# Splitting the loads of x into two 48-row parts and reordering the transform's exchanges, in a fused Fourier, gated and expert-routed kernel

## Chip, cores and metric

One core of a Trainium2 chip runs the kernel. The metric is the device time of one launch, in microseconds (us). Three runs of the kernel before give a median of 3674.27 us.

## What is computed

Three layers follow each other on 8 sequences of 3072 positions with 256 channels each. The first is a Fourier transform along the positions, a complex product with two 256 x 256 matrices, a soft threshold, and the inverse transform:

```python
X = np.fft.rfft(x, axis=1)
Yr = Xr @ w_r - Xi @ w_i + b_r
Yi = Xr @ w_i + Xi @ w_r + b_i
Yr = sign(Yr) * maximum(abs(Yr) - 0.01, 0); Yi likewise
y = np.fft.irfft(Yr + 1j * Yi, n=3072, axis=1)
```

The second is a gated layer on all 24576 tokens, `sigmoid(y @ w_gate) * (y @ w_val) @ w_out`, with an inner width of 1536. The third sends each token whose skip score is above zero to one of 8 experts, chosen by the largest of 8 logits, and adds `gate_w * (relu(z @ w1[e]) @ w2[e])` to it; the other tokens pass through.

## The kernel before

Every matmul operand is a pair of 16-bit halves (a high and a low part), so a product takes three matmuls. The scale of each pair is a power of two found from a maximum: `allpow` takes the maximum of each partition on VectorE, spreads it over the partitions with one small matmul on TensorE (L169, tile `pm`), and reduces that on VectorE.

The forward transform of one sequence is done in two stages. In the first stage the 3072 positions are seen as 48 rows (n) by 64 columns; the 64 columns are two halves (h) of 32, taken 4 at a time, which makes 8 chunks. `load` (L485) brings one chunk of x, 384 KB, into a tile of 96 partitions (2 halves x 48 rows) with 1024 numbers each. The source pattern of this one transfer has the half h outermost, then the 48 rows, then 1024 numbers. For each chunk, `bound` takes the maximum, `scale` and `halve` make the 16-bit pair, `cols` runs the first transform matmuls with the constant `c1` (printed as `c`), and the result `ah` goes to the DRAM buffer `asc` (L524). There are three buffers for chunks of x, so the load of chunk c+3 can be issued once chunk c is used up.

The second stage works on one frequency group at a time. `fetch` (L591) reads 128 KB of `asc` into `al`: 4 parts (r), each with 32 positions (j) of 512 numbers. `freq`, `mix` and `inv` transform, mix and transform back, and `store` (L764) writes 128 KB of the same form to `zsc`. Both exchanges have r outermost and j next: partition r x 32 + j of the tile holds part r, position j. The inverse first stage, `y_gen`, loads chunks `zt` of `zsc` (L799, 384 KB, 96 partitions) and makes `yT`, on which the gated layer works (`moe_gen`, L870 and L903).

All of these transfers are issued in program order by one queue, SP's. The only others here are a few constants on ScalarE's queue and the indirect ones on GpSimd's.

The first sequence (b = 0) is transformed alone, before the gated layer can start; this stretch is called the boot here. Beside it the weights of the gated layer are prepared (`setup_moe_gen`: tiles `raw`, `cm`, `cv`, `wf`, `wgv`, `wo`; the loads of `raw` are L324 and L328). At the end of the boot's transform the kernel issues the first three loads of x for sequence 1, then the first `zt` load, then the next `raw`. After the boot the gated layer's matmuls set the pace, and the transforms of sequences 1 to 7, the routing and the preparation of the experts' weights run as steps of generators between them. `step` runs one step: first what the step before left in `k.late` (among others the matmul and the reduction of `allpow`), then the step's own instructions. The program order is fixed when the kernel is built.

Of the kernel before, what the change touches and what calls it, by code (L numbers as in the profile page):

```python
# [17 lines left out]
N1, N2, NK, HN = 48, 64, 24, 32  # L18
# [17 lines left out]
def make_consts():  # L36
    n1, n2, k1, k2 = (np.arange(v, dtype=np.float64) for v in (N1, N2, NK, 64))

    def hl(a):
        a = np.asarray(a, np.float64) * 64.0  # L40
        hi = a.astype(np.float16)
        lo = (a - hi.astype(np.float64)).astype(np.float16)
        return hi, lo

    th = 2 * np.pi * (((64 * n1[:, None, None] + n2[None, :, None]) * k1) % SEQ) / SEQ
    c1 = np.zeros((2, N1, HN, 2, 2, NK))
    c2 = np.zeros((2, 2, NK, HN, 2, N1))
    w = 4.0 / 3.0
    alt = np.stack([n1 * 0 + 1, 1 - 2 * (n1 % 2)])
    for h in range(2):  # L50
        t = th[:, h * HN:(h + 1) * HN]
        c1[h, :, :, 0, h, :] = np.cos(t)
        c1[h, :, :, 1, h, :] = -np.sin(t)
        c2[0, h, :, :, h, :] = (w * np.cos(t)).transpose(2, 1, 0)
        c2[1, h, :, :, h, :] = (-w * np.sin(t)).transpose(2, 1, 0)
        c1[h, :, :, :, h, 0] = alt.T[:, None, :]
        c2[:, h, 0, :, h, :] = w / 2 * alt[:, None, :]
    c1 = np.stack(hl(c1.reshape(96, HN, 96)), 2)
    c2 = np.stack(hl(c2.reshape(96, HN, 96)), 2)
    ph = 2 * np.pi * ((n2[:, None] * k2) % 64) / 64  # L60
    co, si = np.cos(ph), np.sin(ph)
    sg = np.where(k2 < 32, 1.0, -1.0)
    fx = np.zeros((2, 64, 2, 64))
    for r, (re, im) in enumerate(((co, -si), (si, co))):
        fx[r, :, 0] = re
        fx[r, :, 1] = sg * im
    fi = np.zeros((2, 64, 2, 64))
    fi[0, :, 0] = co.T
    fi[0, :, 1] = si.T
    fi[1, :, 0] = -sg[:, None] * si.T  # L70
    fi[1, :, 1] = sg[:, None] * co.T
    su = np.zeros((2, 64, 128))
    sv = np.zeros((2, 64, 128))
    si = np.zeros((128, 2, 64))
    rows = [(0, 0, q) for q in range(33)] + [(1, 0, q) for q in range(32)]
    rows += [(0, 1, q) for q in range(1, 32)] + [(1, 1, q) for q in range(32)]
    for i, (odd, im, q) in enumerate(rows):
        t = 2 * np.pi * (((24 * odd + 48 * q) * n2) % SEQ) / SEQ
        f = 1.0 if odd == 0 and q in (0, 32) else 2.0
        su[odd, :, i] = -np.sin(t) if im else np.cos(t)  # L80
        sv[odd, :, i] = np.cos(t) if im else np.sin(t)
        si[i, odd] = f * (-np.sin(t) if im else np.cos(t))
    f2 = np.stack([np.stack(hl(m.reshape(128, 128)), 1) for m in (fx, su, sv, fi, si)], 1)
    return {
        "c1": np.ascontiguousarray(c1),
        "c2": np.ascontiguousarray(c2),
        "f2": np.ascontiguousarray(f2),
    }
# [13 lines left out]
def shape_consts():  # L102
    c = make_consts()
    q = np.arange(CT)
    cc = np.arange(NC)
    row = 64 * ((q % 192) // 4)[None, :] + HN * (q // 192)[None, :] + NJ * cc[:, None] + (q % 4)[None, :]
    slot = CT * cc[:, None] + q[None, :]
    ids = np.stack([row, slot], -1).reshape(NC * NT3, 128, 2).transpose(1, 0, 2)
    c["ids"] = np.ascontiguousarray(ids.astype(np.float32))
    p = np.arange(128)  # L110
    first = p[:, None] < np.array([65, 64])
    chk = [(p % HN)[:, None] // NJ == cc[None, :], first, ~first]
    c["chk"] = np.concatenate(chk, 1).astype(np.float32)
    m16 = np.zeros((128, 3, 128), np.float16)
    m16[:, 0] = p[:, None] < p[None, :]
    m16[:, 1] = 1.0
    m16[:, 2] = np.eye(128)
    c["m16"] = m16
    c["m32"] = np.eye(128, dtype=np.float32)
    r = np.zeros((128, 2 * NE + 1 + NBLK), np.float32)  # L120
    r[:, :NE] = np.arange(NE, 0, -1)
    r[:, NE:2 * NE] = np.arange(NE) * NTOK
    r[:, 2 * NE] = p
    r[:, 2 * NE + 1:] = np.arange(NBLK)
    c["rc"] = r
    return c
# [34 lines left out]
def allpow(k, out, in_, lo):  # L161

    p = k.pt.tile([128, 1], F32, tag="pp", name="pp", bufs=6)
    pow2(k, p, in_, lo)

    def spread():
        ps = k.pa.tile([128, 512], F32, tag="pa", name="pm")[:, :128]
        w = p.bitcast(BF16)[:, 1:2].broadcast_to([128, 128])
        k.nc.tensor.matmul(ps, w, k.idb, start=True, stop=True)  # L169
        k.V.tensor_reduce(out, ps, axis=AX.X, op=ALU.max)  # L170

    k.late.append(spread)


def absmax(k, out, in_, axis=AX.X):
# [30 lines left out]
    k.G.tensor_tensor(lo, tmp, hi, op=ALU.subtract)  # L206


def step(k, r):

    k.V.sum = k.S.sum = k.T.sum = k.G.sum = 0.0
    todo, k.late = r[1], []
    for f in todo:
        f()
    got = next(r[0], -1)
    r[1] = k.late
    if got == -1 or isinstance(got, str):
        for f in r[1] if got == -1 else ():
            f()
        return got  # L220
    return max(k.V.sum + k.G.sum, k.S.sum)


def run_all(k, gen):
    r = [gen, []]
    while step(k, r) != -1:
        pass

# [226 lines left out]
def attn_gen(k, b):  # L455
# [23 lines left out]
    def load(i):  # L479

        e, c = b + i // NC, i % NC
        if e < NB:
            xv = k.d.x[e].rearrange("(n h j) d -> h n j d", h=2, j=HN)
            x32[e, c] = k.xp.tile([96, NJ, D], F32, tag="x32", name=f"x32_{e}_{c}")
            nc.sync.dma_start(x32[e, c], xv[:, :, c * NJ:(c + 1) * NJ, :])  # L485

    def bound(c, h=None):
        if h is None:
# [98 lines left out]
    def fetch(g):  # L587
        al = als[g] = k.wp.tile([128, 2, 2, D], F16, tag="al", name=f"al_{b}_{g}", bufs=AL)
        for i, k1 in enumerate(groups[g]):
            src = asc.rearrange("(r q) j l e -> q r j (l e)", r=4)[k1]  # L590
            nc.sync.dma_start(al[:, i].rearrange("p l e -> p (l e)"), src)  # L591

    for g in range(AL):
# [155 lines left out]
    def inv(g):  # L749
        W, yh = len(groups[g]), yhs.pop(g)  # L750
        ps = bank()
        for n, (a, w) in enumerate(PROD):
            k.T.matmul(
                ps[:, :W * D].rearrange("p (a e) -> p a e", a=W), k.f2[:, 4 if g == 0 else 3, a, :], yh[:, :W, w, :],
                start=n == 0, stop=n == 2,
            )
        zh = k.wp.tile([128, 2, 2, D], F16, tag="zh", name="zh")
        pv = ps[:, :W * D].rearrange("p (a e) -> p a e", a=W)

        def store():  # L760
            (split_far if b == 0 else split)(k, zh[:, :W, 0, :], zh[:, :W, 1, :], pv, 2.0**-13)
            for i, k1 in enumerate(groups[g]):
                dst = zsc.rearrange("(r q) j l e -> q r j (l e)", r=4)[k1]
                nc.sync.dma_start(dst, zh[:, i].rearrange("p l e -> p (l e)"))  # L764

        if b == 0:
            k.late.insert(0, store)
        else:
            store()
# [74 lines left out]
def y_boot(k):  # L844
    for c in range(2):
        yield from y_gen(k, 0, c, True)
# [410 lines left out]
def build(tc, d, nb=NB, nstat=NSTAT, dbg=None):  # L1257
# [18 lines left out]
    k.tc, k.nc, k.d, k.nstat = tc, nc, d, nstat  # L1276
    k.due, k.folded = None, False
    k.V, k.S, k.T, k.G = (Meter(e, r) for e, r in ((nc.vector, 960.0), (nc.scalar, 1200.0), (nc.tensor, 2400.0), (nc.gpsimd, 960.0)))
    k.yT, k.st, k.zsc, k.R, k.late = {}, {}, {}, {}, []
    k.x32, k.zt = {}, {}  # L1280
    with ExitStack() as top, tc.manual_schedule():

        def P(name, bufs, space=None, ctx=top, side=None):
            kw = {} if space is None else {"space": space}
            if side is not None:
                kw["side"] = side
            if space is not bass.MemoryType.DRAM:
                kw["reuse_waits"] = "tile"
            return ctx.enter_context(tc.tile_pool(name=name, bufs=bufs, **kw))
# [14 lines left out]
        k.xp = P("xp", 3, ctx=far, side="right")  # L1304
        k.wp = P("wp", 2, ctx=far, side="right")
        k.sp0 = P("sp0", 1, ctx=su)
        ra = [attn_gen(k, 0), []]
        total = step(k, ra)
        setup_consts(k)
        rm = [setup_mix(k), []]  # L1310
        rs = [setup_moe_gen(k), []]
        n, m, more, goal = 0, 0, True, 0.0
        while True:
            w = step(k, ra)
            if w == -1:
                if not more:
                    break
                more = False
                ra = [y_boot(k), []]
                continue  # L1320
            total += w if more else 0.0
            n += 1
# [17 lines left out]
        for c in range(2):  # L1340
            y_scales(k, k.yT[(0, c)][1])
        su.close()
        k.qp = P("qp", 1, ctx=far, side="right")
        k.gp = P("gp", 1, ctx=far, side="right")
        k.rp = P("rp", 2)
# [72 lines left out]

        tasks = {"y": ys, "attn": attns, "route": routes, "prep": lambda: prep_gen(k), "start": starts}
        every = {"y": YSTEP, "attn": 0.0, "route": 3.2, "prep": PSTEP, "start": 1.0}  # L1420
        run = k.run = {n: [[g(), []], 0.0] for n, g in tasks.items()}
        k.made, room, u = {0}, 0.0, 0
        span = spent = 0.0

# [121 lines left out]
```

## Time and profile before

| what | us |
|---|---|
| median of 3 runs (lowest, highest) | 3674.27 (3673.9, 3677.27) |
| the profiled execution | 3679.0 |
| its span (first to last instruction) | 3677.2 |
| TensorE matmul busy in the span | 3401.7 |
| VectorE busy | 2386.7 |
| ScalarE busy | 1634.5 |
| GpSimd busy | 624.7 |

The mean granted TensorE clock of the execution is 0.983 of full speed. Over the span the DMA engines moved 336.04 MB. A busy TensorE is not an engine at its peak, since matmuls are pipelined and their ends are modelled. In the rows below a line such as "12.29 1.22 DVE L144 ... [9.29 <-DMA x<-in_x_dram]" is an instruction that began at 12.29 us and took 1.22 us, on an engine that had been idle for 9.29 us until the named transfer landed. Compute instructions mostly carry L144, the line of a helper that passes them on, and are told apart by their tiles.

### The profile page before, as it was taken

What the parts mean: (1) busy time and instruction counts of PE and PEld (TensorE: products, weight loads), DVE (VectorE), ACT (ScalarE), POOL (GpSimd) and SP (SyncE); (2) the same over time, 40 slices, a digit from 0 to 9 for tenths busy, and PEclk for the clock granted to TensorE, in tenths of its full rate; (3) what the DMA queues carried; (4) which work ended last, traced back from release to release, by engine and by line L of the source; (5) the groups of instructions that cost most, each with busy time, mean ns of one, the idle gap of its engine ahead of it and who ended that gap; (6) DMA issues with size and microseconds to landing.
All of it is one profiled execution on the core that took longest, in us unless ns stands there. A gap on an engine that the chain in (4) does not pass through costs nothing. (4 is left out here: it accounts for less than half of the span.)

```text
span 3677.2 us, 67017 instructions
## 1 busy us (share of the span) xinstructions
PE 3401.7 (93%) x26189; PEld 2429.7 (66%) x26190; DVE 2386.7 (65%) x5583; ACT 1634.5 (44%) x3207; POOL 624.7 (17%) x613
## 2 busy tenths in 40 slices
PE   2728999999999999999999999999999999999997
PEld 1516776676667666766776676666666666667775
DVE  3867667766876776667767776776645455665553
ACT  2434455544545444544444444545444344333332
POOL 1320010022012101110121012101210211433332
PEclk9959999999999999999999999999999999999999
DMA  3422323232322322223222222223210121444442
GB/s 99 134 88 80 112 74 109 82 90 88 110 76 86 92 79 88 74 82 97 77 83 90 88 80 86 77 89 90 57 57 27 40 76 41 143 142 160 155 157 100
DMA packets 214449, 336.04 MB, mean 91 GB/s; under 512 B 31105, under 2 KB 175235, under 8 KB 206864
## 3 DMA queue, kind: packets, MB, share of 16 engines
q1 hardware_dynamic: 197952, 305.40, 26.1%
q0 software_dynamic: 15744, 25.99, 2.3%
q8 instruction: 206, 3.38, 0.4%
q14 instruction: 115, 0.94, 0.1%
q10 hardware_dynamic: 432, 0.33, 0.0%
HBM read 177.99 MB, written 134.09 MB: 85 GB/s over the span
## 5 line engine op out<-in xcount | busy, mean ns | idle before, releaser
L870 PE MATMUL pg<-yT,wgv 128*128 128x384 f16 x9216 | 1634.6, 327 | 2.2 <-ACT sg L144 2.2
L870 PEld LDWEIGHTS <-wgv 128*128 128x128 f16 x9216 | 893.8, 98 | 533.8 <-issue 13.7
L903 PE MATMUL pz<-wo,hh 128*128 128x265 f16 x6912 | 917.9, 277 | 17.9 <-DVE hh L144 15.1
L144 DVE TENSOR_TENSOR hh<-h,hh 128x384 f16<-128x384 f32 x768 | 436.9, 569 | 584.8 <-ACT hh L144 582.8
L903 PEld LDWEIGHTS <-hh 128*128 128x128 f16 x6912 | 675.3, 98 | 211.3 <-DVE hh L144 19.4
L144 ACT ACTIVATE sg<-pg,ys 128x384 f32<-128x384 f32 x768 | 444.4, 579 | 679.8 <-PE pg L870 676.7
L144 DVE SCALAR_TENSOR_TENSOR h<-pg,sg 128x384 f32<-128x384 f32 x768 | 421.9, 549 | 1.4 <-PE pg L870 1.4
L144 ACT CAST hh<-h 128x384 f16<-128x384 f32 x768 | 386.7, 504 | 42.3 <-DVE h L144 41.5
L144 POOL TENSOR_TENSOR x<-sm,x 128x256 f16<-128x256 f32 x77 | 55.0, 714 | 1788.6 <-ACT x L144 832.7
L1000 POOL DMA_INDIRECT lst<-rent,ridx x192 | 201.2, 1048 | 545.7 <-DVE rent L144 277.1
L1225 PE MATMUL ph<-zT,we 128*128 128x512 f16 (+3 forms) x1344 | 268.2, 357 | 4.7 <-DVE h L144 4.1
L1245 PE MATMUL py<-we,h 128*128 128x256 f16 x2400 | 271.0, 273 | 1.0 <-DVE h L144 1.0
L1245 PEld LDWEIGHTS <-h 128*128 128x128 f16 x2400 | 233.5, 98 | 32.7 <-DVE h L144 1.3
L1225 PEld LDWEIGHTS <-we 128*128 128x128 f16 x1344 | 128.0, 98 | 135.8 <-issue 10.5
L144 PEld LDWEIGHTS <-x 128*128 128x128 f16 x1842 | 183.7, 101 | 43.8 <-issue 10.6
L144 ACT ACTIVATE h<-ph 128x512 f16<-128x512 f32 (+3 forms) x224 | 122.3, 548 | 184.6 <-PE ph L1225 182.4
L144 DVE SCALAR_TENSOR_TENSOR h<-ph,h 128x512 f16<-128x512 f32 (+3 forms) x224 | 140.8, 631 | 63.4 <-ACT h L144 61.6
L169 PE MATMUL pm<-idb,pp 128*128 128x128 bf16 x156 | 34.1, 227 | 141.1 <-DVE pp L144 133.5
L144 ACT ACTIVATE ah<-ps 96x512 f16<-96x512 f32 x120 | 70.9, 590 | 162.0 <-PE ps L144 162.0
L1251 POOL DMA_INDIRECT out_dram<-og,ix x100 | 99.6, 996 | 248.3 <-DVE gr L144 70.7
L144 DVE SCALAR_TENSOR_TENSOR og<-py,gr,zg 128x256 f32<-128x256 f32 x100 | 48.3, 483 | 143.9 <-PE py L1245 143.6
L144 PE MATMUL ps<-wri,x 128*128 128x256 f16 x918 | 127.4, 287 | 8.8 <-DVE x L144 7.2
(227 smaller groups left out, 3473.1 us busy)
## 6 DMA issues: line engine op xcount, KB each, us to landing
we<-w SPq DMA_DIRECT2D x56, 1024.0 KB
x<-in_x_dram SPq DMA_DIRECT2D x64, 384.0 KB
asc<-ah SPq DMA_DIRECT2D x64, 384.0 KB
al<-asc SPq DMA_DIRECT2D x192, 128.0 KB
zsc<-zh SPq DMA_DIRECT2D x192, 128.0 KB
zt<-zsc SPq DMA_DIRECT2D x64, 384.0 KB
zs<-zo SPq DMA_DIRECT2D x64, 384.0 KB
yh<-yn SPq DMA_DIRECT2D x308, 64.0 KB
```

The source lines that it names most:

```text
L144: return f(*a, **kw)
L169: k.nc.tensor.matmul(ps, w, k.idb, start=True, stop=True)
L870: nc.tensor.matmul(ps[:, :CT], k.wgv[:, t, g, a, f * 128:(f + 1) * 128], yT[:, t, w, :], start=n == 0, stop=n == 5)
L903: nc.tensor.matmul(zs[(b, c)][t][:, :ZW], hh[:, a, t * 128:(t + 1) * 128], k.wo[:, f, w, :], start=f == 0 and i == 0, stop=f == NF - 1 and ...
L1000: nc.gpsimd.indirect_dma_start(out=k.lst, out_offset=bass.IndirectOffsetOnAxis(ap=idx[:, t:t + 1], axis=0), in_=ent[:, t, :], in_offset=No ...
L1225: k.nc.tensor.matmul(ps, st.w[0][:, a, t * FE + f * 128:t * FE + (f + 1) * 128], st.zT[:, t, w, :], start=m == 0, stop=m == 5,)
L1245: k.nc.tensor.matmul(ps[:, :D], st.h[f][:, a, q * 128:(q + 1) * 128], st.w[1][:, w, f * D:(f + 1) * D], start=n == 0, stop=n == 23,)
L1251: k.nc.gpsimd.indirect_dma_start(out=k.d.out, out_offset=bass.IndirectOffsetOnAxis(ap=st.ix[:, 0, q:q + 1], axis=0), in_=o[:, q], in_offse ...
```

## The change

The load of a chunk of x becomes two transfers of 48 rows, one for each half. The exchanges with `asc` and `zsc` have the position j outermost and the part r next, so that partition 4 x j + r holds part r, position j; the constant matrices of the transform and the mask `chk` are permuted on the host to fit. Third, `allpow`'s matmul and reduction, once the boot is over, are run after a step's own instructions instead of before them (`k.later`); other late work stays ahead.

```diff
+    at = np.arange(128).reshape(2, 2, HN).transpose(2, 0, 1).reshape(128)
+    f2 = [m.reshape(128, 128)[at] for m in (fx, su, sv)] + [m.reshape(128, 128)[:, at] for m in (fi, si)]
+    f2 = np.stack([np.stack(hl(m), 1) for m in f2], 1)
...
-    chk = [(p % HN)[:, None] // NJ == cc[None, :], first, ~first]
+    chk = [(p // 4)[:, None] // NJ == cc[None, :], first, ~first]
...
-    k.late.append(spread)
+    (k.late if k.boot else k.later).append(spread)
...
+def task(gen):
+    return [gen, [], []]
...
     todo, k.late = r[1], []
+    last, k.later = r[2], []
     for f in todo:
         f()
     got = next(r[0], -1)
-    r[1] = k.late
+    for f in last:
+        f()
+    r[1], r[2] = k.late, k.later
...
-            nc.sync.dma_start(x32[e, c], xv[:, :, c * NJ:(c + 1) * NJ, :])
+            for h in range(2):
+                nc.sync.dma_start(x32[e, c][h * N1:(h + 1) * N1], xv[h, :, c * NJ:(c + 1) * NJ, :])
...
-            src = asc.rearrange("(r q) j l e -> q r j (l e)", r=4)[k1]
+            src = asc.rearrange("(r q) j l e -> q j r (l e)", r=4)[k1]
...
-                dst = zsc.rearrange("(r q) j l e -> q r j (l e)", r=4)[k1]
+                dst = zsc.rearrange("(r q) j l e -> q j r (l e)", r=4)[k1]
...
         su.close()
+        k.boot = False
```

On SP's queue at the program's start, before the change (a name such as `x_0_0` is chunk 0 of sequence 0, the shape is that of the destination, and `c` is the first transform's constant):

```order
L485 DMA x_0_0_100<-in_x_dram 96x1x1024
L485 DMA x_0_1_102<-in_x_dram 96x1x1024
L485 DMA x_0_2_104<-in_x_dram 96x1x1024
L257 DMA c_106<-in_c_dram 96x1536 x4
L258 DMA chk<-in_chk_dram 128x12
```

The same place after the change:

```order
L495 DMA x_0_0_100<-in_x_dram 48x1024 x2
L495 DMA x_0_1_103<-in_x_dram 48x1024 x2
L495 DMA x_0_2_106<-in_x_dram 48x1024 x2
L266 DMA c_109<-in_c_dram 96x1536 x4
L267 DMA chk<-in_chk_dram 128x12
```

Each load is now two transfers of 48 partitions, and nothing else has moved in this queue.

On SP's queue at the end of the boot's transform, before the change (`zsc` is written by `store`, `x_1_0` to `x_1_2` are the first chunks of sequence 1, `zt_0` is the first chunk of the inverse stage, `raw` a piece of the gated layer's weights):

```order
L324 DMA raw<-in_moe_w_val_dram 128x1024
L764 DMA zsc_556<-zh 4x32x512 x3
L485 DMA x_1_0_1590<-in_x_dram 96x1x1024
L485 DMA x_1_1_1592<-in_x_dram 96x1x1024
L485 DMA x_1_2_1594<-in_x_dram 96x1x1024
L799 DMA zt_0_1596<-zsc_556 96x2048
L324 DMA raw<-in_moe_w_val_dram 128x1024
```

The same place after the change:

```order
L333 DMA raw<-in_moe_w_val_dram 128x1024
L774 DMA zsc_564<-zh 32x4x512 x3
L495 DMA x_1_0_1598<-in_x_dram 48x1024 x2
L495 DMA x_1_1_1601<-in_x_dram 48x1024 x2
L495 DMA x_1_2_1604<-in_x_dram 48x1024 x2
L809 DMA zt_0_1607<-zsc_564 96x2048
L333 DMA raw<-in_moe_w_val_dram 128x1024
```

The sequence is the same; the stores have 32 positions outermost instead of 4 parts, and six transfers of x instead of three stand ahead of `zt`.

On VectorE at the start of sequence 1's transform, before the change (`px<-pm` is the reduction of `allpow`, `mx<-x` and `px<-x` are maxima of a chunk of x, `hh` and `h` belong to the gated layer):

```order
L144 TENSOR_SCALAR pp<-mx_1897 128x1
L144 TENSOR_SCALAR pp<-pp 128x1
L144 TENSOR_REDUCE px_1896<-pm 128x1
L144 TENSOR_REDUCE mx_1897<-x_1_1_1592 96x1
L144 TENSOR_TENSOR hh<-h_1881,hh 128x384
L144 SCALAR_TENSOR_TENSOR h_1928<-pg,sg 128x384
L144 TENSOR_REDUCE px_1896<-x_1_1_1592 96x1
L144 TENSOR_TENSOR mx_1897<-mx_1897,px_1896 96x1
L144 TENSOR_SCALAR pp<-mx_1897 128x1
L144 TENSOR_SCALAR pp<-pp 128x1
L144 TENSOR_REDUCE px_1896<-pm 128x1
L144 TENSOR_SCALAR px_1896<-px_1896 128x1
```

The same place after the change:

```order
L146 TENSOR_SCALAR pp<-mx_1908 128x1
L146 TENSOR_SCALAR pp<-pp 128x1
L146 TENSOR_REDUCE mx_1908<-x_1_1_1601 96x1
L146 TENSOR_REDUCE px_1907<-pm 128x1
L146 TENSOR_TENSOR hh<-h_1892,hh 128x384
L146 SCALAR_TENSOR_TENSOR h_1939<-pg,sg 128x384
L146 TENSOR_REDUCE px_1907<-x_1_1_1601 96x1
L146 TENSOR_TENSOR mx_1908<-mx_1908,px_1907 96x1
L146 TENSOR_SCALAR pp<-mx_1908 128x1
L146 TENSOR_SCALAR pp<-pp 128x1
L146 TENSOR_SCALAR px_1907<-px_1907 128x1
L146 TENSOR_REDUCE px_1907<-pm 128x1
```

Two reductions of `pm` have each moved behind one instruction. The same two move in each of the sequences 1 to 7; these 14 places are all that differs in VectorE's sequence, and the sequences of TensorE, ScalarE and GpSimd are the same row for row as before.

## Rows read from the trace of the kernel before

**Rows 1.** The page, busy share of TensorE's matmuls in 40 equal slices of the span.
```profile
PE   2728999999999999999999999999999999999997
```

**Rows 2.** Stages: busy us of PE, PEld, DVE, ACT, POOL; PE clock, DMA share, GB/s.
```profile
60.00:80.00 20.00, 5.70 (x26) 4.79 (x27) 9.42 (x19) 6.92 (x12) 4.16 (x4) 1.00 0.31 101
...
160.00:200.00 40.00, 24.29 (x164) 16.37 (x163) 39.33 (x55) 17.24 (x30) 18.17 (x17) 0.77 0.38 122
...
220.00:248.00 28.00, 0.00 (x0) 0.00 (x0) 4.33 (x7) 1.10 (x2) 1.41 (x1) 0.50 0.24 81
...
267.00:300.00 33.00, 26.62 (x178) 16.96 (x179) 20.06 (x54) 12.69 (x23) 0.00 (x0) 0.90 0.15 48
300.00:3600.00 3300.00, 3211.56 (x24827) 2288.94 (x24826) 2175.20 (x5170) 1507.10 (x2978) 539.26 (x529) 1.00 0.29 90
```

**Rows 3.** The same view for three short stretches of the boot.
```profile
238.00:247.00 9.00, 0.00 (x0) 0.00 (x0) 0.00 (x0) 0.00 (x0) 0.00 (x0) 0.50 0.13 51
219.00:222.00 3.00, 0.00 (x0) 0.00 (x0) 2.96 (x6) 1.90 (x3) 1.46 (x2) 0.50 0.27 96
108.00:111.00 3.00, 0.40 (x2) 0.30 (x2) 2.83 (x9) 0.31 (x1) 0.46 (x1) 1.00 1.04 279
```

**Rows 4.** Waits of VectorE up to 250 us: total us, times, longest us.
```profile
DVE mx L144 <- DMA x<-in_x_dram: 33.7, 8, 9.3
```

**Rows 5.** Timeline of the first chunks: start us, us, engine, line, operation.
```profile
0.72 5.65 SPq L485 DMA_DIRECT2D x<-in_x_dram  x3
...
0.95 0.39 ACTq L254 DMA_DIRECT2D m<-in_m_dram  x1
...
2.77 0.23 DVE L144 CAST idb<-m 128x128 bf16<-128x128 f32 x1 [1.70 <-DMA m<-in_m_dram]
...
6.42 14.98 SPq L257 DMA_DIRECT2D c<-in_c_dram  x4
12.29 1.22 DVE L144 TENSOR_REDUCE mx<-x 96x1 f32<-96x1024 f32 x1 [9.29 <-DMA x<-in_x_dram]
...
39.41 0.65 SPq L485 DMA_DIRECT2D x<-in_x_dram  x1
...
43.55 1.22 DVE L144 TENSOR_REDUCE mx<-x 96x1 f32<-96x1024 f32 x1 [5.80 <-DMA x<-in_x_dram]
...
52.12 1.22 DVE L144 TENSOR_REDUCE mx<-x 96x1 f32<-96x1024 f32 x1 [0.71 <-DMA x<-in_x_dram]
```

**Rows 6.** Timeline of the boot's end.
```profile
214.60 0.62 ACT L144 CAST zh<-tmp 128x512 f16<-128x512 f32 x1 [3.15 <-DMA zsc<-zh]
...
220.26 4.40 SPq L485 DMA_DIRECT2D x<-in_x_dram  x3
...
221.53 1.64 DVE L144 SCALAR_TENSOR_TENSOR wf<-raw,cv 128x512 int32<-128x512 int32 x1
...
224.82 1.53 SPq L799 DMA_DIRECT2D zt<-zsc  x1
226.46 7.75 SPq L324 DMA_DIRECT2D raw<-in_moe_w_val_dram  x1
248.87 2.10 PE L144 MATMUL ps<-c,zt 96*128 96x96 f16 x24 [30.92 <-DMA zt<-zsc]
250.11 0.66 ACT L144 ACTIVATE cm<-raw 128x512 f32<-128x512 f32 x1 [28.97 <-DMA raw<-in_moe_w_val_dram]
```

**Rows 7.** Timeline where the second stage of the boot's transform begins.
```profile
112.00 3.45 SPq L591 DMA_DIRECT2D al<-asc  x5
...
117.41 0.38 SPq L328 DMA_DIRECT2D raw<-in_moe_w_out_dram  x1
...
125.71 0.43 DVE L144 TENSOR_SCALAR cm<-cm 128x512 f32<-128x512 f32 x1 [4.53 <-ACT cm L144]
```

**Rows 8.** Waits of TensorE from 400 to 3600 us.
```profile
PE pm L169 <- DVE pp L144: 35.3, 25, 3.1
...
PE ps L144 <- DMA al<-asc: 1.0, 1, 1.0
```

More of the change, by code (lines that the diff above doesn't have):

```diff
@@ L82, in make_consts @@
         si[i, odd] = f * (-np.sin(t) if im else np.cos(t))
-    f2 = np.stack([np.stack(hl(m.reshape(128, 128)), 1) for m in (fx, su, sv, fi, si)], 1)
+    at = np.arange(128).reshape(2, 2, HN).transpose(2, 0, 1).reshape(128)
+    f2 = [m.reshape(128, 128)[at] for m in (fx, su, sv)] + [m.reshape(128, 128)[:, at] for m in (fi, si)]
+    f2 = np.stack([np.stack(hl(m), 1) for m in f2], 1)
     return {
@@ L215, in step @@
     got = next(r[0], -1)
-    r[1] = k.late
+    for f in last:
+        f()
+    r[1], r[2] = k.late, k.later
     if got == -1 or isinstance(got, str):
-        for f in r[1] if got == -1 else ():
+        for f in r[1] + r[2] if got == -1 else ():
             f()
@@ L224, in run_all @@
 def run_all(k, gen):
-    r = [gen, []]
+    r = task(gen)
     while step(k, r) != -1:
@@ L1278, in build @@
     k.V, k.S, k.T, k.G = (Meter(e, r) for e, r in ((nc.vector, 960.0), (nc.scalar, 1200.0), (nc.tensor, 2400.0), (nc.gpsimd, 960.0)))
-    k.yT, k.st, k.zsc, k.R, k.late = {}, {}, {}, {}, []
-    k.x32, k.zt = {}, {}
+    k.yT, k.st, k.zsc, k.R, k.late, k.later = {}, {}, {}, {}, [], []
+    k.x32, k.zt, k.boot = {}, {}, True
     with ExitStack() as top, tc.manual_schedule():
@@ L1306, in build @@
         k.sp0 = P("sp0", 1, ctx=su)
-        ra = [attn_gen(k, 0), []]
+        ra = task(attn_gen(k, 0))
         total = step(k, ra)
         setup_consts(k)
-        rm = [setup_mix(k), []]
-        rs = [setup_moe_gen(k), []]
+        rm = task(setup_mix(k))
+        rs = task(setup_moe_gen(k))
         n, m, more, goal = 0, 0, True, 0.0
@@ L1318, in build @@
                 more = False
-                ra = [y_boot(k), []]
+                ra = task(y_boot(k))
                 continue
@@ L1420, in build @@
         every = {"y": YSTEP, "attn": 0.0, "route": 3.2, "prep": PSTEP, "start": 1.0}
-        run = k.run = {n: [[g(), []], 0.0] for n, g in tasks.items()}
+        run = k.run = {n: [task(g()), 0.0] for n, g in tasks.items()}
         k.made, room, u = {0}, 0.0, 0
```

## The prediction

> **What bounds the kernel now.** I read the page's slices first, then the stages, then the waits inside the stages that are not full. The slices show TensorE at 9 tenths or more from the fourth on, and at 2, 7, 2 and 8 in the first four, which are some 92 us each [rows 1]. The stages say the same in numbers: from 300 to 3600 us TensorE is busy 3211.6 of 3300 us, while in the boot it is busy 5.7 of 20 us at 60 to 80, and not at all at 220 to 248 [rows 2]. So there are two kernels here. After some 270 us TensorE's own work sets the time, and a change that touches only transfers can win no more than TensorE's waits for transfers; that view shows 1.0 us of waiting for `al` in 3200 us, beside 35.3 us for the small spreading matmuls [rows 8]. Before 270 us a chain of transfers and short instructions sets the time, and every us taken from that chain ends the program a us earlier, since the order behind it is fixed.
>
> Who sets the pace in the boot? VectorE waits 33.7 us for loads of x, in 8 waits, one per chunk, the longest 9.3 [rows 4]; the first chunk's maximum begins at 12.29 us, though its load was issued at 0.72 [rows 5]. At 160 to 200 us VectorE itself is the bound, 39.3 of 40 us busy [rows 2]. At the end TensorE idles 30.9 us for the first `zt`, and ScalarE 29.0 us for a piece of weights [rows 6]. SP had issued `zt` at 224.8; it landed 24 us later.
>
> Why so late? Three short stretches in which one kind of transfer runs alone answer it [rows 3]. At 238 to 247 us the three loads of x for sequence 1 are all that is left: a DMA share of 0.13, which is 2.1 of 16 engines, at 51 GB/s. At 219 to 222 only stores to `zsc` run: 0.27, 4.3 engines, 96 GB/s. At 108 to 111 a constant over 96 partitions runs: 1.04, all 16, 279 GB/s. The outermost sizes of these patterns are 2 halves, 4 parts and 96 partitions. The engines that work are as many as the outermost size, up to 16. So a chunk of x takes 393 KB / 51 GB/s = 7.7 us on two engines, and whatever stands behind it in SP's queue has a share on these two and waits: three chunks are 23 us, which is the time that `zt` was late.
>
> **The change, part by part.** With 48 and 32 outermost I take all 16 engines. An engine moved 51 / 2.08 = 24.5 GB/s, so 16 move up to 392 GB/s, against the 279 that the constant reached. A chunk of x then takes 1.0 to 1.4 us, three chunks 3.0 to 4.2, and a 131 KB exchange 0.3 to 0.5 instead of 131 / 96 = 1.4. No row shows an outermost size of 48 or 32; from below the bound is the 4 engines of the exchanges.
>
> The Trainium skill, page "DMA: Bandwidth & Descriptors", section "Why a DMA increments its semaphore by 16 and not by 1", says that a transfer is cut over the largest number up to 16 that divides the outermost sizes of both sides. The trace agrees for 2 and 4 [rows 3]; by that rule 48 and 32 both give 16, and the sum below stands.
>
> *The eight chunks.* A small load, `m`, was issued at 0.95 us and its reader began at 2.77, so 1.8 us go from issue to landing beside the data [rows 5]. Six issues at 0.35 us (`m`'s was 0.39) stand at the head of SP's queue. The first chunk, whose two parts are issued by 1.4 us, lands by about 4.2 instead of 12.3. VectorE is idle from 3.0, so 1.2 of the first wait is left. The other seven waits fall if each later load lands before VectorE gets there. Without waits a chunk takes VectorE 52.12 - 0.71 - 43.55 = 7.9 us [rows 5]. The load of chunk 4, issued at 39.41, was wanted at 43.55 + 7.9 = 51.4, 12 us later, and needs 0.7 + 1.4 + 1.8 = 3.9. So all seven go. What could be late next is the constant `c`, issued behind the six loads: 1.2 MB of x and 1.2 MB of `c` at 279 GB/s are done at some 11 us, and the first matmul would want it near 13. Gain 33.7 - 1.2, less half a us for small things: 32 us, bounds 28 (if each chunk gives back half a us) and 33.
>
> *The boot's end.* Six issues take 2 us, so `zt` is issued at about 222.3 instead of 224.8. Three chunks ahead of it end at 224.5, `zt`'s own data takes 1.0, and it lands at about 227 instead of 248.9: 22 us. The weights behind it (512 KB) need their buffer, free when VectorE's instruction at 221.53 ends, 223.2; they land near 228 instead of 250.1, again 22 us [rows 6]. From there on both chains go as before. Upper bound 24, if only that buffer counts (223.2 + 1.3 + 1.8 = 226.3); lower 16, if parts of 48 rows go at half the rate and `raw` queues behind them.
>
> *The exchanges in the boot.* The five first fetches of `al` are issued at 112.0 and take 5 x 1.4 us on four engines; the weights issued at 117.41 land late behind them, and VectorE idles 4.5 us for it [rows 7]. At 214.6 ScalarE waits 3.2 us for a `zsc` store before the last stores [rows 6]. Both waits go with short exchanges, but TensorE has other work in the first, and VectorE is full in the stage between. I take 4 us; bounds 0 and 8.
>
> *The rest.* In sequences 1 to 7 the same transfers lie under TensorE's work, and 1.0 us of waiting is all there is to win [rows 8]. SP gets 64 more issues; a load of x took 0.65 us to issue [rows 5], two at 0.35 take 0.7. The third edit moves no matmul: TensorE's sequence is unchanged, and 14 reductions of `pm` come one instruction later, behind a maximum of half a chunk (about half of the 1.22 us in rows 5) or a one-column instruction. Their readers are a step away. I cost this at nothing; uncovered it would be 7 x 0.6 = 4 us.
>
> The sum: 32 + 22 + 4 = 58 us. The profiled execution took 3679.0 for a span of 3677.2; the median is 4.7 below it. 3674.3 - 58 = 3616 us. TensorE runs at half clock at 220 to 248 and at 0.90 over 267 to 300 [rows 2]; a half-clock stretch that moves with the work may shift some 3 us either way.
>
> **The rivals.** *Parts on few engines.* If 48 rows use, say, 4 engines, a chunk takes 3.9 us: the first wait falls by 4, the others still go (28 in all), `zt` gains 11, the exchanges as above: 43 us, 3631. Nothing in the trace excludes it. Chance 0.10.
>
> *The loads do not get faster.* The split puts the same bytes on the same queue; if the halves shared the two engines, or went one after the other at the old rate, only the exchanges' 4 us and the landing of first halves would be left: about 3669, which is within 0.2% (7 us), what a measurement of this kernel can tell from no change. The stretch at 0.13 speaks against it: 14 engines stand idle. Chance 0.05. The Trainium skill, the same page, section "Rules for kernel authors", says so in general: two transfers to disjoint partition halves aren't worth making, since they serialize on the same engines. Here the single transfer used 2.1 of them [rows 3], a case that the rule doesn't have in view.
>
> *Slower: the exchanges' pieces jump.* With r outermost an engine ran through 32 positions that lie next to each other in DRAM; with j outermost each 1 KB piece lies 24 x 32 KB from the next. At 96 GB/s on 4.3 engines a piece takes 46 ns; after, an engine has 8 of them per exchange, so they may take 4 times as long before an exchange is as slow as now. The 48 exchanges of the boot lie between 112 and 223 us; they fill that stretch at 2.3 us each, or 290 ns a piece, and eat the whole gain of 54 at 3.4 us, or 430 ns. At 600 ns (4.8 us each) the time would be 3674 - 54 + 48 x 2.5 = 3740. Loads of x in 4 KB pieces with jumps run at 24.5 GB/s an engine, so jumps alone don't show here. Chance 0.04.
>
> **How the numbers follow.** The forecast's case has 0.81: the bounds of its terms give 28 + 16 + 0 - 3 = 41 to 33 + 24 + 8 + 3 = 68 us of gain, 3606 to 3633. The few-engines case, 3631, lies in it too; the two others are left out. I widen the fast side by 2. Faster by over 0.2% is 0.91, within it 0.05, slower 0.04.
>
> **What would show it.** The first maximum near 4 us; VectorE's wait for x down from 33.7 to 2; the eighth chunk's maximum 32 us earlier; a DMA share near 1 while x loads; TensorE's wait for `zt` at 9 us or less; the gated layer's first matmul some 58 us earlier; the same 3211 of 3300 us afterwards. Wrong would be: a new wait for `c` or for weights that takes the place of x, a share of 0.25 while x loads, or exchanges that take over 2 us.

## The result, and the profile after

The changed kernel took 3616.87 us (median of 4 runs, 3615.93 to 3617.13) against 3675.77 for the kernel before on the same chip (4 runs, 3673.9 to 3679.04): ratio 0.9838, 95% interval 0.9821 to 0.9855, 58.9 us less. On another chip, beside experiments 5 to 7, it was 3621.44 against 3685.29, ratio 0.9826 (0.9813 to 0.9839), 63.9 us less. The forecast was 58 us.

The profiled execution after took 3615.93 us, with a span of 3614.1; the one before was 3679.0, itself 3.2 above its median, so the two traces differ by 63 us where the medians differ by 58.9. These are the slices and the stages of the changed kernel, with the columns of [rows 1, 2]:

```profile
PE   3669999999999999999999999999999999999997
```

```profile
40.00:60.00 20.00, 7.89 (x33) 5.77 (x32) 12.06 (x22) 11.53 (x20) 5.66 (x5) 1.00 0.40 113
...
120.00:160.00 40.00, 21.48 (x167) 14.96 (x166) 39.37 (x56) 17.24 (x30) 17.21 (x16) 0.85 0.41 126
...
220.00:250.00 30.00, 23.88 (x164) 15.70 (x165) 19.26 (x45) 10.70 (x19) 0.00 (x0) 0.89 0.18 50
...
300.00:3600.00 3300.00, 3211.09 (x24884) 2289.66 (x24882) 2155.30 (x5132) 1496.14 (x2968) 550.46 (x545) 1.00 0.30 91
```

TensorE's full stretch begins one slice earlier; inside it nothing changed: 3211.1 of 3300 us busy, as before [rows 2]. VectorE is full at 120 to 160, as it was at 160 to 200. So the gain lies ahead of the full stretch. The first chunks, from the timeline, and VectorE's wait for x (total, times, longest; [rows 4, 5] before):

```profile
0.72 3.63 SPq L495 DMA_DIRECT2D x<-in_x_dram  x6
...
5.18 4.20 SPq L266 DMA_DIRECT2D c<-in_c_dram  x4
5.29 1.22 DVE L146 TENSOR_REDUCE mx<-x 96x1 f32<-96x1024 f32 x1 [0.76 <-DMA x<-in_x_dram]
...
51.99 1.20 DVE L146 TENSOR_REDUCE mx<-x 96x1 f32<-96x1024 f32 x1
```

```profile
DVE mx L146 <- DMA x<-in_x_dram: 0.8, 1, 0.8
```

The first maximum begins at 5.3 us instead of 12.3. The eighth begins at 52.0 without a wait; before it began at 84.0, as the view of the tile `mx` says (first and last start):

```profile
L144 DVE TENSOR_REDUCE mx<-x x8: 1216/1216/1216, 12.3 to 84.0; 96x1 f32<-96x1024 f32 x8
```

The start of the second stage and the boot's end ([rows 6, 7] before), from the timeline:

```profile
80.06 3.46 SPq L601 DMA_DIRECT2D al<-asc  x5
...
89.78 0.43 DVE L146 TENSOR_SCALAR cm<-cm 128x512 f32<-128x512 f32 x1 [0.54 <-ACT cm L146]
...
173.42 0.62 ACT L146 CAST zh<-tmp 128x512 f16<-128x512 f32 x1 [1.50 <-DMA zsc<-zh]
...
179.10 2.92 SPq L495 DMA_DIRECT2D x<-in_x_dram  x6
...
182.12 0.37 SPq L809 DMA_DIRECT2D zt<-zsc  x1
...
188.22 2.10 PE L146 MATMUL ps<-c,zt 96*128 96x96 f16 x24 [11.46 <-DMA zt<-zsc]
189.35 0.67 ACT L146 ACTIVATE cm<-raw 128x512 f32<-128x512 f32 x1 [9.82 <-DMA raw<-in_moe_w_val_dram]
...
206.45 6.57 PE L880 MATMUL pg<-yT,wgv 128*128 128x384 f16 x30
```

The program order is the same on both sides, so the difference between two starts of the same instruction says how far the boot had run ahead by then. The fetches of `al` are 31.9 us earlier (112.00 to 80.06), VectorE's `cm` 35.9, the loads of x for sequence 1 41.2 (220.26 to 179.10), the first matmul on `zt` 60.7 (248.87 to 188.22), the gated layer's first matmul 60.8 (it began at 267.20 before). The chunks gave 32, the second stage 9, the boot's end 19.5, and the span after it 2.4.

How the transfers ran, in a short stretch in which VectorE does next to nothing and the loads of x, `zt` and `raw` are under way (columns of [rows 3]):

```profile
183.00:186.00 3.00, 0.00 (x0) 0.00 (x0) 0.07 (x1) 0.00 (x0) 0.00 (x0) 0.50 1.03 234
```

All 16 engines work, where 2.1 did, and they move 234 GB/s, where two moved 51.

### The profile page after: what moved, and what is told of

It reads as the page before. It is cut to its first block, busy times and chain, and to the rows that moved or that the text cites. A ratio compares the mean times of both kernels' runs of the same rounds, so it can differ in the third digit from the quotient of the medians.

```text
span 3614.1 us, 67120 instructions
## 1 busy us (share of the span) xinstructions
PE 3391.1 (94%) x26190; PEld 2423.8 (67%) x26190; DVE 2385.8 (66%) x5583; ACT 1633.8 (45%) x3207; POOL 620.2 (17%) x613
## 4 chain that ended last, share of the span: by engine, by line
PE 78%; DVE 13%; ACT 4%; issue 3%; DMA 2%; POOL 1%; SPq 0%; DVEq 0%; ACTq 0%; POOLq 0%
PE pg L880 35%; PE pz L913 18%; PE ps L146 11%; PE py L1255 7%; PE ph L1235 6%; DVE h L146 1%; DVE hh L146 1%; DVE ys L146 1%; DVE px L146 1%; DVE xh L146 1%; DVE yf L146 1%; ACT hh L146 1%; ACT xh L146 1%; ACT sg L146 1%; DVE pp L146 1%
```

## The experiments

Each was compared with the kernel before on its own chip; chips differ by some 15 us, so the ratios are compared, or medians taken side by side on one chip. In experiments 1 to 4 the kernel before took 3690.36 us (18 runs).

**1. Only the loads of x.** The kernel before with this edit alone:

```diff
-            nc.sync.dma_start(x32[e, c], xv[:, :, c * NJ:(c + 1) * NJ, :])
+            for h in range(2):
+                nc.sync.dma_start(x32[e, c][h * N1:(h + 1) * N1], xv[h, :, c * NJ:(c + 1) * NJ, :])
```

Expected: 

> Only the loads of x are split; exchanges and spreading matmuls are as before. Theory (the outermost size of a transfer sets how many engines carry it, and the boot waits for x): the eight chunks give 32 us and the boot's end 19 to 20, so about 52 us less than before, some 3624 us, with VectorE's wait for x under 2 us and the wait for weights before the second stage (5 us) still there. Rival (the gain comes as much from the exchanges, which unblock the boot's end): half of it, 25 to 30 us, near 3648.

Measured: 3637.86 us, ratio 0.9858 (0.9843 to 0.9874), 52.5 us less. The wait for the first `zt` is the 31 us of [rows 6] cut to 13, with exchanges as slow as before:

```profile
197.13 2.10 PE L144 MATMUL ps<-c,zt 96*128 96x96 f16 x24 [12.94 <-DMA zt<-zsc]
```

This matmul began 51.7 us earlier than before. The theory holds; the rival's 25 to 30 us is out.

**2. Only the exchanges.** The kernel before with `"q j r (l e)"` in both exchanges and the permuted constants; x loaded as before.

Expected: 

> Only the exchanges have the position outermost; x is loaded as before. Theory: the second stage of the boot gives 5 to 9 us, so 3667 to 3671 us, and the 31 us wait for the first inverse chunk stays, since the loads of x still stand ahead of it on two engines. Rival (1 KB pieces that jump cost as much as the added engines give): no gain or a loss, 3675 us or more.

Measured: 3679.82 us, ratio 0.9974 (0.9963 to 0.9984), 10.5 us less (6 to 14 by the interval), where 5 to 9 were expected. The waits of TensorE for `zt` and of VectorE for x stay (total, times, longest):

```profile
PE ps L146 <- DMA zt<-zsc: 30.7, 1, 30.7
```

```profile
DVE mx L146 <- DMA x<-in_x_dram: 33.8, 8, 9.3
```

The 1 KB pieces that jump through DRAM cost nothing that shows: by the packet records of the traces a piece takes 46 ns (median) here, in the kernel before and in the changed one. The rival falls.

**3. Only the spreading step.** The changed kernel with loads and exchanges as before, so that `(k.late if k.boot else k.later).append(spread)` and `step` are all that is left of the change.

Expected: 

> Only the spreading step is run at a step's end. Theory: 14 reductions move by one instruction, no matmul moves, so 3675 us, within 2 us of before. Rival (the moved reductions release TensorE's banks later or earlier, which shows as waits of the spreading matmuls): 4 us or more either way.

Measured: 3689.33 us, ratio 0.9998 (0.9989 to 1.0007). It does nothing to the time. It does change how waits read. Waits of TensorE's spreading matmuls from 400 to 3600 us, first in the kernel before, then here:

```profile
PE pm L169 <- DVE pp L144: 35.3, 25, 3.1
...
PE pm L169 <- DVE px L144: 4.7, 3, 1.9
```

```profile
PE pm L169 <- DVE pp L144: 29.2, 21, 3.0
...
PE pm L169 <- DVE px L144: 10.9, 7, 2.2
```

35.3 + 4.7 and 29.2 + 10.9 are both 40: four waits have another last releaser, since VectorE's reduction now stands after a maximum, and the sum is the same.

**4. One transfer per chunk, rows outermost.** The changed kernel with

```diff
-            xv = k.d.x[e].rearrange("(n h j) d -> h n j d", h=2, j=HN)
+            xv = k.d.x[e].rearrange("(n h j) d -> n h j d", h=2, j=HN)
...
-            for h in range(2):
-                nc.sync.dma_start(x32[e, c][h * N1:(h + 1) * N1], xv[h, :, c * NJ:(c + 1) * NJ, :])
+            nc.sync.dma_start(x32[e, c], xv[:, :, c * NJ:(c + 1) * NJ, :])
```

and the rows of the first constant in the same order.

Expected: 

> The changed kernel, but a chunk of x is one transfer again, with the 48 rows outermost and the half next (the rows of the constant of the first transform matmuls are permuted to fit). Theory: 16 engines carry it as they carry the two parts, so the time is that of the changed kernel, 3615 to 3618 us, or a us or two less for half as many issues. Rival (it is the split into two transfers that lets them overlap, not the outermost size): the x gain is lost and only the exchanges' stays, near 3668 us.

Measured: 3626.49 us, ratio 0.9822 (0.9809 to 0.9836), against 0.9838 and 0.9826 of the changed kernel. It is the outermost size, not the split, that brings the engines in. The Trainium skill's rule on disjoint partition halves (page "DMA: Bandwidth & Descriptors", section "Rules for kernel authors") holds in this form: two halves are no faster than one transfer that has 48 outermost.

In experiments 5 to 8, on another chip, the kernel before took 3685.29 us (9 runs) and the changed one, **8**, 3621.44 (5 runs).

Expected of 8: 

> The changed kernel unaltered, beside the others on this chip, as their measure: ratio 0.982 to 0.986 to the kernel before.

**5. The kernel before, loads behind `zt`.**

```diff
     if b == 0:
-        for c in range(NC, NC + 3):
-            load(c)
+        k.first = lambda: [load(c) for c in range(NC, NC + 3)]
...
         zt_load(k, b, c, boot)
+        if boot and c == 1:
+            k.first()
```

Expected: 

> The kernel before, with one thing moved: the first three loads of x for sequence 1 are issued behind the second load of zt instead of ahead of the first. Theory (the first zt was late because it stood behind three loads on two engines): the wait of 31 us falls to some 8, 20 to 24 us less than before, ratio 0.9935 to 0.9946, with loads of x no faster. Rival (zt was late for the stores to zsc that it waits for, or the weights would be late anyway): under 5 us, ratio above 0.9985.

Measured: 3669.48 us, ratio 0.9952 (0.9939 to 0.9966), 15.8 us less, short of the 20 to 24 expected. The trace has the whole gain at `zt`, and shows where a third of it went again:

```profile
226.39 2.10 PE L144 MATMUL ps<-c,zt 96*128 96x96 f16 x24 [9.14 <-DMA zt<-zsc]
...
256.58 0.43 DVE L144 TENSOR_TENSOR se<-w 128x256 f32<-128x256 f32 x1 [7.31 <-DMA w<-in_w_i_dram]
```

The first matmul on `zt` is 22.5 us earlier than in [rows 6], so position in the queue was the cause, as the theory has it. But the loads of x still use two engines for 23 us, and what stands behind them now is a weight `w` that VectorE wants: it waits 7.3 us where it did not before, and TensorE then idles 7.7 us, until 259.5, in the gated layer, whose first matmul had begun 22.6 us earlier. The stall was moved, and a smaller one came in its place.

**6. The changed kernel with the same move.**

Expected: 

> The changed kernel with the same move. Theory (the 6 us from zt's issue to its landing are still the three chunks ahead of it, now on 16 engines): zt and the weights land some 4 us earlier, 4 us less than the changed kernel. Rival (6 us is what a load takes there by itself): the same time as the changed kernel.

Measured: 3616.42 us, 5.0 less than the changed kernel beside it; ratio to before 0.9809 (0.9796 to 0.9823). `zt` was issued at 180.86 us and landed 3.8 later, against 6.1 behind the three chunks:

```profile
180.86 0.34 SPq L808 DMA_DIRECT2D zt<-zsc  x1
...
184.63 2.10 PE L146 MATMUL ps<-c,zt 96*128 96x96 f16 x24 [7.62 <-DMA zt<-zsc]
```

**7. Experiments 4 and 6 together.**

Expected: 

> Both at once: one transfer of x with the 48 rows outermost, and the move. Theory: the two don't touch each other; 4 us less than the changed kernel from the move, and 0 to 2 from half the issues. If the single transfer alone was faster than two parts for another reason, it shows here as more than 6 us.

Measured: 3616.59 us, ratio 0.9812 (0.9798 to 0.9825), the same as 6 within 0.2 us. Half as many issues are worth nothing here. By the ratio, 6 and 7 are the fastest versions that were run.

**9. Parts of 24 rows.** The changed kernel with four transfers per chunk:

```diff
             for h in range(2):
-                nc.sync.dma_start(x32[e, c][h * N1:(h + 1) * N1], xv[h, :, c * NJ:(c + 1) * NJ, :])
+                for n in range(0, N1, 24):
+                    o = h * N1 + n
+                    nc.sync.dma_start(x32[e, c][o:o + 24], xv[h, n:n + 24, c * NJ:(c + 1) * NJ, :])
```

Expected: 

> The changed kernel with each half of a chunk cut once more: four transfers of 24 rows. Theory (the engines of a transfer are the largest number up to 16 that divides the outermost sizes): 12 engines, a DMA share near 0.75 while x loads alone at the boot's end; since the chunks are still there long before they are wanted, the time stays within 4 us of the changed kernel, ratio 0.982 to 0.985. Rival (any outermost size of 16 or more gets all 16 engines): a share near 1. Rival (more transfers cost issue time on SP that the boot feels): 5 us or more slower than the changed kernel.

Measured: 3631.28 us against 3688.23, ratio 0.9843 (0.9825 to 0.986), which lies in the theory's range. By the changed kernel's two ratios, 0.9838 and 0.9826, that is 2 or 6 us behind it, and the intervals overlap. From 19 to 20 us the four parts of chunk 3 are the only transfers under way:

```profile
19.00:20.00 1.00, 0.98 (x5) 0.53 (x3) 0.64 (x2) 0.33 (x1) 0.00 (x0) 1.00 0.79 146
```

```profile
0.72 9.26 SPq L497 DMA_DIRECT2D x<-in_x_dram  x12
```

The share is 0.79, near 12 of 16 engines, as the theory said; by the packet records mostly 12 pieces are in flight at once. More transfers do cost: twelve issues hold SP for 9.3 us, where six took 3.6, VectorE waits 4.0 us for the first chunk instead of 0.8, and the gated layer's first matmul begins at 211.98 us, 5.5 later than in the changed kernel's trace. How much of that comes from issues and how much from the four engines that are missing was not separated, and whether the time is behind by less than the theory's 4 us or by the rival's 5 is not decided.

## Why the prediction was right, point by point

**What bounds.** The split into a boot set by transfers and a full stretch set by TensorE held. The gain stands complete at the gated layer's first matmul, but for 2 us. (A slip in the reading of [rows 1]: TensorE is at 9 tenths from the fifth slice on, not the fourth.) That an us taken from the boot's chain ends the program an us earlier held for this change, but not in experiment 5, where a third of it was lost at the weights behind.

**Engines by the outermost size.** Right for the sizes of this change: 2 outermost gives a share of 0.13 and 4 gives 0.27; 48 gives 1.03, as 96 did [rows 3], and a single transfer with 48 outermost costs the same as two (experiment 4). For 32 this stretch shows it, in which only stores to `zsc` run:

```profile
172.00:172.75 0.75, 0.00 (x0) 0.00 (x0) 0.71 (x3) 0.00 (x0) 0.00 (x0) 0.50 1.01 352
```

At 352 GB/s an exchange's 131 KB take 0.4 us, as forecast. The sentence that as many engines work as the outermost size, up to 16, is too simple: it gives 16 for 24 rows, and the share there was 0.79, near 12, the largest number up to 16 that divides 24 (experiment 9).

**The eight chunks: 32 forecast, 31.9 measured.** All seven later waits fell, and 0.8 us of the first was left where 1.2 was forecast. The same maximum comes a us later than forecast (5.3 against 4.2) because another small wait grew: VectorE now waits 3.2 us for `m`, 1.5 more; that `m` now shares more engines with x was not tested.

**The exchanges in the boot: 4 forecast, 9.2 measured.** This term was mis-sized, and between these two traces its bounds of 0 to 8 were too narrow. 4.0 us came where the weights no longer stand behind five fetches (31.9 to 35.9), as named, though I had marked that wait as partly hidden. About 2 came from shorter waits for `zsc`, 1.50 instead of 3.15, and what follows them. The remaining 3.3 I had not seen: TensorE's matmuls became fast earlier (last section). Experiment 2 has the same pieces without any change of x: TensorE's matmuls begin 1.9, then 5.7, then 7.8 us earlier than before behind the three places. Experiment 1, with the old exchanges, gains 1.6 us in all that stage (its loads of x for sequence 1 are issued at 186.51, 33.8 us earlier, after 32.2 at the eighth chunk), which is within the spread between runs: from the first matmul on `al` to the last one before `zt` the four traces with the old exchanges take 95.8 to 98.4 us, the kernel before the longest, and the seven with the new ones 89.1 to 90.7, the changed kernel the shortest. So the exchanges are worth some 7 us, and 2 to 3 of the 9.2 belong to this pair of traces.

**The boot's end: 22 forecast, 19.5 measured.** The mechanism is right (experiments 1, 5 and 6); the rate was too high. I let 16 engines move 392 GB/s, from two engines' 24.5 each, and 279 at the slow end; they moved 234. So `zt` landed 6.1 us after its issue instead of 4.7, and its issue, forecast 2.0 us after the first of x, came 3.0 after it. TensorE's wait for `zt` is 11.5 us, where 9 or less was forecast. Experiment 6 shows that the three chunks ahead of `zt` still cost 4 to 5 us: its wait is 7.6, and its median 5.0 lower.

**The rest.** The third edit did nothing (experiment 3). Inside the full stretch TensorE's wait of 1.0 us for `al` [rows 8] is gone.

**The sum.** 58 forecast; 58.9 on the first chip, 63.9 on the second. In the two traces the terms add up to 63: errors of +5 and -2.5, and 2 after the boot, cancel only in part. The medians lie 4 us closer together than these two executions, so that 58 is met within a us on the first chip is luck of some 5 us.

**The rivals.** Parts on few engines: out by the share of 1.03. Loads that get no faster: out by experiment 1. Exchanges that lose by jumping pieces: out by experiment 2.

## What to carry to other kernels

Here a DMA share that stayed near 1/8 or 1/4 while one kind of transfer ran alone went with a pattern that has 2 or 4 outermost, and sizes of 32, 48 and 96 brought in all 16 engines. Look for such a share, and put a multiple of 16 outermost, by the order of one transfer if possible: two parts cost nothing that was measured, four cost issue time. Such a transfer hurt most by what stands behind it in the same queue, so look for the long wait that ends with a transfer issued just after it, and try the queue's order as well as the pattern. Price the mended transfer by a row in which all 16 engines work, not by sixteen times what two of them reach; here such rows read 234 to 352 GB/s, so take the same kind of transfer.

## What the runs showed of the hardware that was not expected

With two engines at work each moved 24.5 GB/s (51 GB/s at 0.13 [rows 3]); with all 16 on 4 KB pieces of x, `zt` and `raw`, 234 GB/s at 1.03, which is 14.2 each. Stores of 1 KB pieces to `zsc` on all 16 kept their pace: 352 GB/s at 1.01, 21.8 each, against 96 at 0.27 [rows 3], 22.2 each. So a share of 1 means that engines are occupied, not that they run at the pace they have alone; why these loads slow down and the stores do not was not tested.

TensorE's clock rose much earlier after the change, and the column of the granted clock does not show it. In the second stage of the boot a matmul of 256 columns took 421 ns and a new one began every 213 ns in the kernel before, up to 137.0 us; from then on it took 273 ns, and one began every 109. In the changed kernel this happened at 90.1 us. The column reads 1.00 on both sides, but before that point it is no reading: in all eleven traces the records of the clock begin within 1 us of the first matmul at the fast pace, and the column counts a time without a record as full speed. Where 0.50 is on record, later in the same trace, the matmul is slow too. Three stretches of the kernel before (columns of [rows 2]), the same matmul in each of them (shortest, median and longest ns), and then after the change:

```profile
134.00:136.00 2.00, 2.00 (x11) 1.44 (x10) 1.12 (x5) 1.82 (x4) 0.63 (x1) 1.00 0.60 184
139.00:141.00 2.00, 2.00 (x20) 1.78 (x19) 1.41 (x3) 0.72 (x2) 0.02 (x1) 1.00 0.27 81
183.20:187.00 3.80, 3.80 (x19) 2.57 (x20) 3.70 (x6) 1.02 (x2) 2.06 (x3) 0.50 0.19 66
```

```profile
L144 PE MATMUL ps<-wri,x x11: 421/421/421, 133.8 to 135.9; 128*128 128x256 f16 x11
...
L144 PE MATMUL ps<-wri,x x20: 272/273/273, 138.8 to 140.9; 128*128 128x256 f16 x20
...
L144 PE MATMUL ps<-wri,x x19: 393/418/418, 183.2 to 187.0; 128*128 128x256 f16 x19
```

```profile
L146 PE MATMUL ps<-wri,x x22: 272/272/273, 95.2 to 97.5; 128*128 128x256 f16 x22
```

A start every 213 ns for 256 columns is 1.2 columns a ns, the lower of the two levels (1.2 GHz), and 109 ns is near the upper (2.4 GHz). So TensorE ran at half clock until the rise in both boots, and the changed one had it 47 us earlier, while it had run 36 us ahead.

In the kernel before TensorE idled twice while ScalarE and VectorE were late behind the weights [rows 7]; after that it worked without a wait until the clock rose:

```profile
126.31 0.61 PE L144 MATMUL ps<-wri,x 128*128 128x256 f16 x2 [0.65 <-ACT x L144]
...
127.91 2.32 PE L144 MATMUL ps<-wri,x 128*128 128x256 f16 x10 [1.00 <-DVE x L144]
```

In the changed kernel its last wait ahead of the rise ended at 85.6 us. The traces tie the earlier rise to the exchanges, but loosely. With the old ones and the old loads the first long stretch at full clock, 30 us or more, begins at 137.0, 132.3 and 133.0 us (the kernel before, experiments 3 and 5, which run the same boot up to there); with the new exchanges and the old loads it begins at 127.2 (experiment 2). What in TensorE's activity brings the rise was not isolated.
